# Scan and gated MLP on one core: two pairs turned by DMA instead of TensorE, and loads and stores moved to GpSimd's queue

## The chip, the cores and the metric

One core of a Trainium2 chip. The metric is the device time of one execution in microseconds (us), as the median of several runs. The profile is one execution taken apart by the hardware profiler; its times are counted from the start of its span. Engines go by the profile's names: PE is TensorE's matmul, PEld its weight load, DVE is VectorE, ACT is ScalarE, POOL is GpSimd, SP is SyncE, which computes nothing here and issues DMAs.

## What is computed

A state-space scan over 4 batches, 8 heads and 768 positions (head width 32, state width 16), then a gated MLP over the 3072 tokens of 256 features:

```
for each chunk c of the positions:
    cum = cumsum(log a)                         # within the chunk
    M = (C B^T) * exp(cum_i - cum_j) * causal
    y = M x + (C state) * exp(cum_i)
    state = exp(sum log a) * state + sum_j B_j x_j exp(cum_last - cum_j)
tokens = y, heads side by side                  # 3072 x 256
out = (relu(tokens w_gate) * (tokens w_val)) w_out   # d_ff = 1536
```

Inputs and output are float32; the kernel multiplies in bf16.

## The kernel before, in words

The scan works in 12 pairs (p), each of two chunks of 128 positions (i = 0, 1) of one batch, all 8 heads at once; three pairs make a batch. The MLP works in 6 blocks (b) of 512 tokens, so block b needs pairs 2b and 2b + 1. In the loop over blocks (lines 968 to 1136), P = 2b + 2, Q = 2b + 3 and W = 2b + 1: while block b goes through the MLP, the pairs of the next block go through the scan. Each engine executes its instructions in the order of the program (`in_order`, line 15); that order is written out by hand, so whatever stands behind a waiting instruction waits too. DMAs issued by SP go through one queue and those issued by GpSimd through another.

A pair passes these steps:

- **Load** (`load`, line 102): C and B (two DMAs each of 64 KB in rows of 64 bytes, for pairs from 4 on) and x (two of 128 KB in rows of 128 bytes). The raw tiles have four buffers each.
- **Scaling**: B and C are multiplied by the decay factors `fac`. Pairs 0 to 5 use `scale_bc` or `scale_one` (lines 334 and 348) into a tile `bs`. Pairs 6 to 11 use `scale_padded` (line 292), which writes a zeroed tile `bz` (three of them, used in turn) with B in part 0, all of C in part 1 and C split by even and odd heads in parts 2 and 3.
- **Turning**, positions to heads x states. Pairs up to 5: `turn` (line 912), four TensorE transposes (line 389) into PSUM, then `tevac`: ScalarE copies B (`BT`, line 318), VectorE scales C twice with 0/1 masks (`CT`, line 415). Pairs from 6 on: one DMA transpose of the `bz` tile on SP's queue (`TT`, line 306).
- **x cast** to bf16 (`to_x`, line 358), on GpSimd or ScalarE.
- **G** = B C^T on TensorE (line 452, or 491 from pair 6 on) into four PSUM banks; **gevac** (line 458) moves it to the tile `gs` with the causal mask. ScalarE copies half q = 0 and part of q = 1, GpSimd masks these in place (`causal`, line 171, two instructions for a pair), VectorE does the rest.
- **inter** (lines 619, 670): C times the carried state; **Dm** (lines 630, 683): `gs` times x, into y. Dm waits for the masks of GpSimd. **states** (lines 569, 698) sums B^T x for the next pairs.
- **yevac** writes y to `yT`, the MLP's input.

Pairs from 6 on take G, inter and Dm two pairs at a time. In the MLP, `gv` and `gvh` compute gate and value products (lines 743, 758), ScalarE applies relu, VectorE multiplies, `fout` (line 788) makes the output product and `foevac` (line 806) copies it to an `ob` tile and stores it from SP.

What stands around the change on GpSimd, in order: in block 0, masks of pairs 2 and 3, scalings of pair 4 (`scale_one`, line 353); in block 1, C of pair 4, scaling of pair 5 (line 344) and its x cast, scaling of pair 6 (line 297, two copies of line 303) and its x cast, masks of pair 4, masks of pair 5, scaling and x cast of pair 7; in block 2, the small state products (`Sn`, line 722), scaling and x cast of pair 8, scaling of pair 9, masks of pair 6, masks of pair 7, state products. SP issues, from block 0's end: C of pair 4, a store, C, B and x of pair 5, a store, all of pair 6, all of pair 7, the transpose of pair 6, all of pair 8, two stores, the transpose of pair 7, all of pair 9, the transposes of pairs 8 and 9.

Of the kernel before, what the change touches and what calls it, by code (L numbers as in the profile page):

```python
# [11 lines left out]
ALU = mybir.AluOpType  # L12
# [17 lines left out]
def kernel(  # L30
# [13 lines left out]
    nc = tc.nc  # L44

    NB, NH, S, D = x.shape
    N = B.shape[-1]
# [26 lines left out]
    def place(p):  # L74
        b, c0 = p // PPB, 2 * (p % PPB)
        return b, c0, slice(c0 * 128, (c0 + 2) * 128)
# [215 lines left out]
    def scale_padded(p, eng):  # L292

        b, c0, _ = place(p)
        z = turned[p % 3]
        f = fac[:, b, c0:c0 + 2].rearrange("s i j h -> s i (j h)")
        eng.tensor_tensor(  # L297
            out=z.rearrange("s (i k) (h n) -> s i (k h) n", k=4, n=N)[:, :, 0:2 * NH],
            in0=st[p]["bcr"].rearrange("s i j h n -> s i (j h) n"),
            in1=f.to_broadcast([128, 2, 2 * NH, N]), op=ALU.mult)  # L300
        parts = z.rearrange("s (i k) (q t n) -> s i k t q n", k=4, q=4, t=2)
        for t in range(2):
            eng.tensor_copy(out=parts[:, :, 2 + t, t], in_=parts[:, :, 1, t])
        st[p]["B"] = [z[:, 4 * i] for i in range(2)]
        tt = st[p]["TT"] = att.tile([128, 8, 128], BF16, tag="TT", name="TT", bufs=4)
        nc.sync.dma_start_transpose(out=tt, in_=z.rearrange("s k n -> s (k n)"))

    def new_bs(p):
        st[p]["bs"] = att.tile([128, 4, 128], BF16, tag="bs", name="bs", bufs=6)
# [38 lines left out]
    def scale_one(p, eng, j):  # L348

        b, c0, _ = place(p)  # L350
        for i in range(2):
            f = fac[:, b, c0 + i, j].rearrange("s (t q) -> s t q", t=2)
            eng.tensor_tensor(
                out=st[p]["bs"][:, 2 * i + j].rearrange("s (q t n) -> s t q n", q=4, t=2),
                in0=st[p]["bcr"][:, i, j].rearrange("s (t q) n -> s t q n", t=2),
                in1=f.to_broadcast([128, 2, 4, N]), op=ALU.mult)
# [60 lines left out]
    def ct(p, i, rows=slice(0, 128), t=None):  # L417
        if p < NWIDE:
            c = st[p]["CT"][rows, :, :, 64 * i:64 * i + 64]
        else:  # L420
            c = st[p]["CT"][rows, :, i]
        return c if t is None else c[:, t]

    def split(p, ap):

        return ap.rearrange("s t (r m) -> s t r m", r=2) if p < NWIDE else ap
# [17 lines left out]
    def G(p):  # L444
        s = st[p]
        if "gp" not in s:
            G_banks(p)
        g = s["gp"]
        for i in range(2):
            for q in range(4):  # L450
                r = slice(32 * q, 32 * q + 32)
                nc.tensor.matmul(  # L452
                    out=split(p, g[q][:, i]), lhsT=s["BT"][r, i], rhs=ct(p, i, r),
                    start=(i == 0), stop=True, tile_position=(32 * q, 0),
                    skip_group_check=True)
        s["gs"] = att.tile([128, 4, 4, 128], BF16, tag="gs", name="gs", bufs=2)
# [336 lines left out]
    def fout_last(b):  # L793

        r0 = b * 512 + 384
        for m in range(2):
# [6 lines left out]
            (nc.vector.tensor_copy if m else nc.scalar.copy)(out=ob, in_=o)  # L803
            (nc.sync if m else nc.scalar).dma_start(out=out[r0:r0 + 128, ms], in_=ob)

    def foevac(b, ts, o=None):
        last = b == NBLK - 1 and ts == 2
        if ts % 2 == 0 and not last:
            return
        ob = ffn.tile([128, 2, DM], FP32, tag="ob", name="ob", bufs=3)  # L810
        r0 = b * 512 + ts * 128
        if last:
            nc.scalar.copy(out=ob[:, 0], in_=fst["o"][:, 0])
            nc.scalar.dma_start(out=out[r0:r0 + 128, :], in_=ob[:, 0])
            return
        nc.scalar.copy(out=ob, in_=o or fst["o"])  # L816
        rows = out[r0 - 128:r0 + 128, :].rearrange("(i p) m -> p i m", p=128)
        for part in ((slice(0, 1), slice(1, 2)) if b in (2, 3) and ts == 3 else (slice(0, 2),)):
            nc.sync.dma_start(out=rows[:, part], in_=ob[:, part])


    B_, C_ = slice(0, 1), slice(1, 2)
# [145 lines left out]
    for b in range(NBLK):  # L968
        P, Q, W = 2 * b + 2, 2 * b + 3, 2 * b + 1
        more = P < NPAIR  # L970
        if b == 1:
            load(P + 2, nc.sync)
            load(P + 3, nc.sync)
        if b == 2:
            scale(Q, nc.gpsimd)
            load(Q + 2, nc.sync)

        nh = (4, 6, 8, 0)[min(b, 3)]
        for f in range(nh):
            if b == 0:  # L980
                continue
            turning = f == (3 if b == 1 else nh - 3)
            gvh_mm(b, f, 0)
            gvh_relu(b, f, 0)
            gvh_mul(b, f, 0)
            if b == 1 and f == 1:
                to_x(P, nc.scalar)
            if turning:
                inter(W, 0)
                inter(W, 1)  # L990
                Dm(W)
                if b == 1:
                    states(P)
                    scale_one(P, nc.gpsimd, 1)
                else:
                    states_two((P, Q))
                yevac(W, nc.scalar)
                if b == 1:
                    spread(P)
                else:  # L1000
                    sums_two((P, Q))
        for f in range(nh):
            gvh(b, f, 1)
        if b == 2:
            scale(P + 2, nc.gpsimd)
        for f in range(nh, NF):
            gv(b, f, b > 2 and f == 0)
            if b == 0:
                if f == 5:
                    over_sum(de_ps)  # L1010
                if f == 7:
                    sevac(1, 1)
                if f == 9:
                    turn(P)
                    tevac(P, nc.scalar, nc.vector)
                if f == 10:
                    held(Q, bc=False)
                if f == 11:
                    back(P)
                    backevac(P, nc.scalar)  # L1020
            elif b == 1:
                if f == nh:
                    turn(P)
                    tevac(P, nc.scalar, nc.vector)
                    scale(Q, nc.gpsimd)
                if f == 8:
                    turn(Q)
                    tevac(Q, nc.scalar, nc.vector)
                    scale(Q + 1, nc.gpsimd)
                    load(Q + 3, nc.sync)  # L1030
            elif b == 2:
                if f == 9:
                    scale_padded(Q + 2, nc.gpsimd)
                    load(Q + 3, nc.sync)
                    load(Q + 4, nc.sync)
            elif b == 3:
                if f in (2, 6):
                    scale(P + 2 + f // 4, nc.gpsimd)
# [3 lines left out]
        if b == 0:  # L1042

            for third in range(3):
# [16 lines left out]
                if third == 1:  # L1061
# [11 lines left out]
            A_ps[0] = rest  # L1073
            Dm(P)
            states(Q)
            held(Q + 2)
            fout(b, 3, range(4))
            inter(P, 0)
            inter(P, 1)
            gevac(Q, after={2: lambda: [yevac_half(P, t, nc.scalar) for t in range(2)],  # L1080
                            3: lambda: spread(Q)})
            new_bs(Q + 1)
            scale_one(Q + 1, nc.gpsimd, 0)
            fout(b, 3, range(4, NF))
            foevac(b, 3)
            continue
        elif b == 1:
            fout(b, 0)
            G(P)
            gevac(P)  # L1090
            over_sum2(de)
            fout(b, 1)
            foevac(b, 1)
            fout(b, 2)
        elif more:
            ahead = (P + 2, Q + 2) if Q + 2 < NPAIR else ()
            fout(b, 0, range(9), True)
            G_rows(P)
            opened = y_banks()
            inter_rows(P, opened)  # L1100
            inter_rows(Q, opened)
            gevac(P)
            fout(b, 0, range(9, NF))
            fout(b, 1)
            first_two = fst["o"]
            fout(b, 2, range(1))
            G_rows(Q)
            gevac(Q)
            if b == 2:
                to_x(Q + 2, nc.scalar)  # L1110
            foevac(b, 1, first_two)
            fout(b, 2, range(1, NF))
            fout(b, 3, range(8))
            Dm_two((P, Q))
            states_two(ahead)
            yevac_two((P, Q))
            sums_two(ahead)
            fout(b, 3, range(8, NF))
            foevac(b, 3)
            continue  # L1120
# [48 lines left out]
```

## Time and profile before

| | |
|---|---|
| median of 3 runs | 121.95 us (121.88 to 122.23) |
| the profiled execution | 121.95 us |
| its span, first to last instruction | 120.2 us |
| PE busy | 115.2 us, 96% of the span |
| DVE, ACT, POOL busy | 88.2, 76.7, 51.0 us |
| DMA traffic | 13.69 MB in 80591 packets, 73424 of them under 512 bytes |
| granted TensorE clock | 1.000 |

The page gives busy shares, the span in 40 slices of 3 us with the busy share in tenths, the chain of work that ended last followed back from the end, and the costliest groups of instructions. The timeline lists one engine's instructions in order of time, neighbours of a kind merged; in square brackets stands the idle time before them and what seems to have ended it. The table by stretches gives, for each stretch, the busy time of each engine, the granted clock, the DMA share (packet time over the time of 16 engines, which passes 1 where packets overlap) and GB/s. A wait for several semaphores is put down to one of them, which need not be the one that held it.

### The profile page before, as it was taken

What the parts mean: (1) busy time and instruction counts of PE and PEld (TensorE: products, weight loads), DVE (VectorE), ACT (ScalarE), POOL (GpSimd) and SP (SyncE); (2) the same over time, 40 slices, a digit from 0 to 9 for tenths busy, and PEclk for the clock granted to TensorE, in tenths of its full rate; (3) what the DMA queues carried; (4) which work ended last, traced back from release to release, by engine and by line L of the source; (5) the groups of instructions that cost most, each with busy time, mean ns of one, the idle gap of its engine ahead of it and who ended that gap; (6) DMA issues with size and microseconds to landing.
All of it is one profiled execution on the core that took longest, in us unless ns stands there. A gap on an engine that the chain in (4) does not pass through costs nothing.

```text
span 120.2 us, 3321 instructions
## 1 busy us (share of the span) xinstructions
PE 115.2 (96%) x1230; PEld 74.8 (62%) x1237; DVE 88.2 (73%) x208; ACT 76.7 (64%) x168; POOL 51.0 (42%) x103
## 2 busy tenths in 40 slices
PE   7988999999999999999999999999999999999990
PEld 2445854677885577887578544578444677444790
DVE  5898879976899866899775787856787775678400
ACT  4257887787998726888626776535767445767240
POOL 6879999744405181956055261633400033000000
PEclk9999999999999999999999999999999999999999
DMA  3999999989959897999995799942200002200022
GB/s 70 209 182 148 202 193 207 211 126 132 163 53 194 98 125 107 135 140 212 126 177 113 72 129 116 281 95 87 87 5 0 0 0 93 87 0 0 0 87 87
DMA packets 80591, 13.69 MB, mean 114 GB/s; under 512 B 73424, under 2 KB 80576, under 8 KB 80576
## 3 DMA queue, kind: packets, MB, share of 16 engines
q1 hardware_dynamic: 73088, 10.54, 54.6%
q0 software_dynamic: 4080, 2.36, 13.9%
q10 hardware_dynamic: 3408, 0.59, 2.6%
q8 instruction: 9, 0.15, 0.5%
q14 instruction: 6, 0.05, 0.1%
HBM read 11.12 MB, written 3.15 MB: 119 GB/s over the span
## 4 chain that ended last, share of the span: by engine, by line
PE 93%; DVE 3%; issue 1%; ACT 0%
PE o L788 26%; PE gate L743 19%; PE val L743 19%; PE gv L758 13%; PE w L200 3%; PE g L491 2%; PE g L452 2%; DVE bs L344 1%; PE y L683 1%; PE y L630 1%; PE o L800 1%; PE tp L389 1%; PE y L619 1%; PE bt L433 1%; PE dw L236 0%
## 5 line engine op out<-in xcount | busy, mean ns | idle before, releaser
L747 DVE TENSOR_TENSOR h<-r,val 128x512 bf16<-128x512 bf16 x54 | 36.9, 686 | 9.1 <-ACT r L746 6.6
L746 ACT ACTIVATE r<-gate 128x512 bf16<-128x512 f32 x54 | 32.2, 597 | 11.9 <-PE gate L743 11.2
L788 PE MATMUL o<-wo,h 128*128 128x256 bf16 x276 | 33.8, 273 | 0.0
L743 PE MATMUL gate<-yT,wg 128*128 128x512 bf16 x105 | 32.0, 379 | 0.2
L743 PE MATMUL val<-yT,wv 128*128 128x512 bf16 x105 | 31.5, 379 | 0.2
L788 PEld LDWEIGHTS <-h 128*128 128x128 bf16 x276 | 25.7, 98 | 5.4 <-issue 1.2
L171 POOL TENSOR_SCALAR_AFFINE_SELECT gs<-gs 128x512 bf16<-128x512 bf16 (+1 forms) x24 | 12.2, 531 | 20.7 <-ACT gs L464 20.7
L475 DVE TENSOR_TENSOR gs<-g,masks 128x512 bf16<-128x512 f32 x24 | 15.4, 685 | 6.0 <-PE g L491 2.8
L743 PEld LDWEIGHTS <-wv 128*128 128x128 bf16 x108 | 10.5, 98 | 12.6 <-DMA wv<-in_moe_w_val_dram 0.3
L743 PEld LDWEIGHTS <-wg 128*128 128x128 bf16 x108 | 10.4, 98 | 11.1
L768 DVE TENSOR_TENSOR h<-r,gv 128x256 bf16<-128x256 bf16 x36 | 14.2, 417 | 1.3 <-ACT r L765 1.1
L765 ACT ACTIVATE r<-gv 128x256 bf16<-128x256 f32 x36 | 13.6, 388 | 1.2
L464 ACT CAST gs<-g 128x512 bf16<-128x512 f32 x12 | 7.0, 586 | 11.4 <-PE g L491 5.8
L758 PE MATMUL gv<-yT,wg 128*128 128x256 bf16 x72 | 13.9, 273 | 0.0
L758 PE MATMUL gv<-yT,wv 128*128 128x256 bf16 x72 | 13.9, 273 | 0.0
L297 POOL TENSOR_TENSOR bz<-bcr,fac 128x512 bf16<-128x512 f32 x6 | 6.3, 1058 | 11.9 <-DMA bcr<-in_B_dram 6.8
L816 ACT COPY ob<-o 128x512 f32<-128x512 f32 x11 | 6.5, 590 | 4.2 <-PE o L788 4.1
L318 ACT CAST yT<-y 128x256 bf16<-128x256 f32 (+1 forms) x11 | 5.4, 515 | 4.9 <-PE y L683 2.8
L758 PEld LDWEIGHTS <-wv 128*128 128x128 bf16 x72 | 7.0, 98 | 0.9
L758 PEld LDWEIGHTS <-wg 128*128 128x128 bf16 x72 | 6.7, 98 | 1.0 <-issue 0.2
L318 POOL CAST xb<-xr 128x512 bf16<-128x512 f32 (+1 forms) x8 | 4.7, 592 | 3.9 <-DMA xr<-in_x_dram 3.9
L200 PE MATMUL w<-const-bfloat16-1.0 128*128 128x512 bf16 (+3 forms) x14 | 5.0, 482 | 0.8 <-PEq L1153 0.8
(120 smaller groups left out, 110.4 us busy)
## 6 DMA issues: line engine op xcount, KB each, us to landing
xr<-in_x_dram SPq DMA_DIRECT2D x24, 128.0 KB, 3.3
out_dram<-ob SPq DMA_DIRECT2D x9, 256.0 KB, 2.5
bcr<-in_B_dram SPq DMA_DIRECT2D x16, 64.0 KB, 3.0
bcr<-in_C_dram SPq DMA_DIRECT2D x16, 64.0 KB, 3.0
wg<-in_moe_w_gate_dram POOLq DMA_DIRECT2D x6, 128.0 KB, 4.8
wv<-in_moe_w_val_dram POOLq DMA_DIRECT2D x6, 128.0 KB, 5.1
wo<-in_moe_w_out_dram POOLq DMA_DIRECT2D x3, 256.0 KB, 6.8
out_dram<-ob SPq DMA_DIRECT2D x4, 128.0 KB, 2.2
```

Of the source, the lines that this page charges most:

```text
L171: nc.gpsimd.affine_select(out=dst, in_=dst, pattern=pattern, compare_op=ALU.is_ge, fill=0.0, base=0, channel_multiplier=-1)
L200: nc.tensor.matmul(out=w[:, 0:cols], lhsT=nc.const_aps.tensor(1.0, [128, 128], BF16), rhs=nc.const_aps.tensor(1.0, [128, cols], BF16), sta ...
L318: (eng.copy if eng is nc.scalar else eng.tensor_copy)(out=out, in_=in_)
L464: nc.scalar.copy(out=d[:, 0], in_=g[0])
L475: nc.vector.tensor_tensor(out=d[:, q], in0=g[q], in1=m, op=ALU.mult)
L743: nc.tensor.matmul(out=o, lhsT=w_tile(ws, f, k), rhs=yT[:, k, tk], start=(k == 0), stop=(k == 1), skip_group_check=True)
L746: nc.scalar.activation(r, g, AF.Relu)
L747: nc.vector.tensor_tensor(out=fst[b][:, f], in0=r, in1=v, op=ALU.mult)
L758: nc.tensor.matmul(out=gv_[:, j], lhsT=w_tile((wgs, wvs)[j], f, k), rhs=yT[:, k, tk], start=(k == 0 and not (early and j)), stop=(k == 1), ...
L765: nc.scalar.activation(r[:, 0:256], fst[b, f, u][:, 0], AF.Relu)
L768: nc.vector.tensor_tensor(out=fst[b][:, f, u * 256:(u + 1) * 256], in0=fst.pop((b, f, u, "r"))[:, 0:256], in1=fst.pop((b, f, u))[:, 1], op ...
L788: nc.tensor.matmul(out=o[:, ts % 2], lhsT=fst[b][:, f, ts * 128:(ts + 1) * 128], rhs=wo[:, f], start=(f == 0 and new), stop=(f == NF - 1), ...
```

## The change

- Pairs 4 and 5 are scaled by a new `scale_turned` into the padded `bz` tiles (four GpSimd instructions for a pair: B by even and odd heads, then C by even and odd heads) and turned by a DMA transpose on SP's queue. Their `turn` and `tevac` go; G, inter and states read `TT` and `bz`.
- GpSimd issues three stores (both of block 0 and the last of block 1, that one held back to block 2) and x of pairs 6 and 8.
- On GpSimd, the x cast of pair 6 moves from ahead of the masks of pair 4 to behind them, and the x cast of pair 8 from ahead of pair 9's scaling to between the masks of pairs 6 and 7.
- SP issues the transpose of pair 4 between B and x of pair 5, and that of pair 5 behind B of pair 6. Stores of blocks 2 to 5 go out in halves.

The core of the diff:

```
+    def scale_turned(p, eng):
+        b, c0, _ = place(p)
+        z = turned[p % 3]
+        dst = z.rearrange("s (i k) (q t n) -> s i k t q n", k=4, q=4, t=2)
+        src = st[p]["bcr"].rearrange("s i j (t q) n -> s i j t q n", t=2)
+        f = fac[:, b, c0:c0 + 2]
+        for j in range(2):
+            for t in range(2):
+                eng.tensor_tensor(
+                    out=dst[:, :, j * (2 + t), t], in0=src[:, :, j, t],
+                    in1=f[:, :, j, 4 * t:4 * t + 4].to_broadcast([128, 2, 4, N]), op=ALU.mult)
+        st[p]["B"] = [z[:, 4 * i] for i in range(2)]
+    def turn_padded(p):
         tt = st[p]["TT"] = att.tile([128, 8, 128], BF16, tag="TT", name="TT", bufs=4)
-        nc.sync.dma_start_transpose(out=tt, in_=z.rearrange("s k n -> s (k n)"))
+        nc.sync.dma_start_transpose(out=tt, in_=turned[p % 3].rearrange("s k n -> s (k n)"))
...
-        for part in ((slice(0, 1), slice(1, 2)) if b in (2, 3) and ts == 3 else (slice(0, 2),)):
-            nc.sync.dma_start(out=rows[:, part], in_=ob[:, part])
+        if b == 1 and ts == 3:
+            late_store.append(lambda: nc.gpsimd.dma_start(out=rows, in_=ob))
+            return
+        for part in ((slice(0, 1), slice(1, 2)) if b > 1 else (slice(0, 2),)):
+            (nc.sync if b else nc.gpsimd).dma_start(out=rows[:, part], in_=ob[:, part])
...
         if b == 1:
-            load(P + 2, nc.sync)
+            new_bc(P + 2)
+            load_bc(P + 2, 1, nc.sync)
+            load_bc(P + 2, 0, nc.sync)
+            scale_turned(Q, nc.gpsimd)
+            turn_padded(Q)
+            new_x(P + 2)
+            for i in range(2):
+                load_x(P + 2, i, nc.gpsimd)
             load(P + 3, nc.sync)
+            to_x(Q, nc.gpsimd)
         if b == 2:
             scale(Q, nc.gpsimd)
+            late_store.pop()()
+            new_x(P + 2)
+            for i in range(2):
+                load_x(P + 2, i, nc.gpsimd)
             load(Q + 2, nc.sync)
...
         if b == 2:
-            scale(P + 2, nc.gpsimd)
+            scale_padded(P + 2, nc.gpsimd)
...
-                if f == nh:
-                    turn(P)
-                    tevac(P, nc.scalar, nc.vector)
-                    scale(Q, nc.gpsimd)
                 if f == 8:
-                    turn(Q)
-                    tevac(Q, nc.scalar, nc.vector)
-                    scale(Q + 1, nc.gpsimd)
-                    load(Q + 3, nc.sync)
+                    scale_padded(Q + 1, nc.gpsimd)
+                    new_bc(Q + 3)
+                    load_bc(Q + 3, 1, nc.sync)
+                    load_bc(Q + 3, 0, nc.sync)
...
-            held(Q + 2)
+            held(Q + 2, with_x=False)
...
-            new_bs(Q + 1)
-            scale_one(Q + 1, nc.gpsimd, 0)
+            scale_turned(Q + 1, nc.gpsimd)
+            turn_padded(Q + 1)
+            new_x(Q + 2)
+            for i in range(2):
+                load_x(Q + 2, i, nc.sync)
...
             G(P)
             gevac(P)
+            to_x(P + 2, nc.gpsimd)
...
             first_two = fst["o"]
+            if b == 2:
+                to_x(P + 2, nc.gpsimd)
             fout(b, 2, range(1))
             G_rows(Q)
             gevac(Q)
```

More of the change, by code (lines that the diff above doesn't have):

```diff
@@ L304, in scale_padded @@
         st[p]["B"] = [z[:, 4 * i] for i in range(2)]
+        turn_padded(p)
+    def scale_turned(p, eng):
[11 more added lines that the diff above has]
+    def turn_padded(p):
         tt = st[p]["TT"] = att.tile([128, 8, 128], BF16, tag="TT", name="TT", bufs=4)
-        nc.sync.dma_start_transpose(out=tt, in_=z.rearrange("s k n -> s (k n)"))
+        nc.sync.dma_start_transpose(out=tt, in_=turned[p % 3].rearrange("s k n -> s (k n)"))
     def new_bs(p):
@@ L420, in ct @@
         else:
-            c = st[p]["CT"][rows, :, i]
+            c = st[p]["TT"][rows, 4 * i + 2:4 * i + 4]
         return c if t is None else c[:, t]
@@ L452, in G @@
                 nc.tensor.matmul(
-                    out=split(p, g[q][:, i]), lhsT=s["BT"][r, i], rhs=ct(p, i, r),
+                    out=split(p, g[q][:, i]), rhs=ct(p, i, r),
+                    lhsT=s["BT"][r, i] if p < NWIDE else s["TT"][r, 4 * i],
                     start=(i == 0), stop=True, tile_position=(32 * q, 0),
@@ L804, in fout_last @@
             (nc.sync if m else nc.scalar).dma_start(out=out[r0:r0 + 128, ms], in_=ob)
+    late_store = []
     def foevac(b, ts, o=None):
@@ L993 @@
                     states(P)
-                    scale_one(P, nc.gpsimd, 1)
                 else:
```

## The prediction

> **What bounds the kernel now.** I read the page first: the busy shares and the chain of work that ended last.
>
> ```profile
> PE 115.2 (96%) x1230; PEld 74.8 (62%) x1237; DVE 88.2 (73%) x208; ACT 76.7 (64%) x168; POOL 51.0 (42%) x103
> ...
> DMA  3999999989959897999995799942200002200022
> ...
> PE 93%; DVE 3%; issue 1%; ACT 0%
> ```
>
> TensorE carries 93% of the chain, so time taken from its stream counts in full, and time taken from VectorE or ScalarE counts only where TensorE waits for them. The waits of TensorE and its weight loads from 16 us on hold nothing over 0.3 us in one place. The DMA row is the second thing to see: it stands mostly at 8 or 9 from 3 us to 63 us. The transfers have little room in the blocks that the change touches.
>
> Next, the timeline of TensorE around the two turns that go (columns: start, duration, engine, line, operation; durations overlap, so a step is the distance from one start to the next).
>
> ```profile
> 36.49 0.59 PE L743 MATMUL val<-yT,wv 128*128 128x512 bf16 x2
> 36.92 0.39 PE L389 MATMUL tp<-ident,bs 128*128 128x128 bf16 x4
> 37.15 0.59 PE L743 MATMUL gate<-yT,wg 128*128 128x512 bf16 x2
> ...
> 38.87 0.39 PE L389 MATMUL tp<-ident,bs 128*128 128x128 bf16 x4
> 39.09 0.59 PE L743 MATMUL gate<-yT,wg 128*128 128x512 bf16 x2
> ```
>
> The turns take 37.15 - 36.92 = 0.23 us and 39.09 - 38.87 = 0.22 us, with no idle time around them.
>
> **The change, part by part.**
>
> Removed from TensorE: eight transposes of pairs 4 and 5 (the built order of instructions has 16 rows fewer on PE, eight weight loads and eight matmuls): 0.23 + 0.22 = **0.45 us** of the chain. G, inter and states of the two pairs read other tiles with the same counts and columns: nothing.
>
> Removed beside it: two BT copies on ScalarE (0.37 us each) and four CT scalings on VectorE (0.34 us each). TensorE runs at its full pace of 0.43 us for two 512-column matmuls behind both turns, so this is worth nothing now.
>
> GpSimd's arithmetic: four L353 scalings (0.40 us) and two L344 scalings (0.62 us), 2.8 us, become eight of L353's size, 3.2 us. The B half of pair 4 is still written first, before the states of block 1 at 32.36 us (0.76 us from 29.94 us on): nothing.
>
> GpSimd's DMA issues: three stores and four x loads, seven in all. Its weight loads (L153) held the engine for 0.776 and 0.739 us each. The store rows, 256 of 1 KB, are like those; the first fits into the idle 1.55 us ahead of the masks at 28.93 us, the second into the wait of 4.51 us for B of pair 5. An x load has 1024 rows of 128 bytes, which no GpSimd row shows: from 0.78 us (the issue alone counts) to 3.1 us (four times the rows). I take 1 us, since the three L161 loads with twice the bytes cost the same 0.770 us, and SP's own issue of x, with a median of 0.62 us, is short too. The Trainium skill ("DMA: Bandwidth & Descriptors", Anatomy of one DMA — SWDGE (gpsimd) path) holds that many descriptors can be issued before their cost shows; by it the term would stay near the lower end, and no run here shows it yet.
>
> The two new DMA transposes: two undisturbed ones of before, issued at 75.77 and 77.18 us and landing 3.2 and 2.9 us later, are 1.1 us apart at landing. So each takes some **1.1 us of the stream of transfers**, 2.2 us together. Their own deadlines hold: that of pair 4 stands behind the B loads of pair 5 in SP's queue, is issued near 34 us and lands within 5.1 us (the longest of before), by 39 us; inter needs it at 41.24 us. That of pair 5 is issued near 40.7 us, lands by 45.8 us at the latest, and G needs it at 46.74 - 0.45 = 46.29 us.
>
> What the 2.2 us push back matters at two places, both on GpSimd, where a scaling that waits for a load stands ahead of the masks that TensorE needs. Block 1:
>
> ```profile
> 41.76 1.06 POOL L297 TENSOR_TENSOR bz<-bcr,fac 128x512 bf16<-128x512 f32 x1 [2.41 <-DMA bcr<-in_B_dram]
> 42.88 0.52 POOL L303 COPY bz<-bz 128x128 bf16<-128x128 bf16 x2
> 43.56 0.61 POOL L318 CAST xb<-xr 128x512 bf16<-128x512 f32 x1 [0.16 <-DMA xr<-in_x_dram]
> 44.45 1.00 POOL L171 TENSOR_SCALAR_AFFINE_SELECT gs<-gs 128x512 bf16<-128x512 bf16 x2 [0.28 <-ACT gs L464]
> ```
>
> B of pair 6 lands at 41.6 us (38.83 + 2.8). Scaling to masks done takes 0.16 + 1.64 + 1.00 = 2.8 us behind it, since the cast moves behind the masks. Dm of pair 4 starts at 46.37, with the gain at 45.92 us. So it is hidden while B lands by **43.1 us**. Ends: 41.6 + 1.1 (one transpose) - 1.4 (two stores out of SP's queue, 0.64 and 0.86 us of issue with what lies between) = 41.3; with everything in one stream, x of pair 6 (1.9 us from B's landing to x's) ahead of it too, 44.6 us. Block 2:
>
> ```profile
> 61.27 1.06 POOL L297 TENSOR_TENSOR bz<-bcr,fac 128x512 bf16<-128x512 f32 x1 [5.13 <-PE y L670]
> 62.39 0.52 POOL L303 COPY bz<-bz 128x128 bf16<-128x128 bf16 x2
> 62.87 1.01 POOL L171 TENSOR_SCALAR_AFFINE_SELECT gs<-gs 128x512 bf16<-128x512 bf16 x2
> 64.24 1.00 POOL L171 TENSOR_SCALAR_AFFINE_SELECT gs<-gs 128x512 bf16<-128x512 bf16 x2 [0.36 <-ACT gs L464]
> ```
>
> The view names PE, but the scaling of pair 9 starts 0.2 us after its B load lands (58.19 + 2.9 = 61.1 us), and no late PE instruction touches its tiles, so I read it as that load. The new cast of x of pair 8 stands between the two pairs of masks: load to last mask is 0.2 + 1.60 + 0.97 + 0.57 + 1.00 = 4.35 us. The last mask is needed by the fourteenth of the 32 matmuls at 65.59 us, near 65.84, or 65.39 us with the gain. So here B must land by **61.05 us**: there is no slack if the load stays where it was. Ends: 61.1 + 2.2 = 63.3 us, if all transfers share one stream; with x of pairs 6 and 8 and the stores gone from SP's queue and costing it nothing, some 57 us.
>
> Which end? This table shows stretches with and without GpSimd's own queue in use (its weight loads run in the first); the last two numbers are the DMA share and GB/s.
>
> ```profile
> 11.50:16.00 4.50, 4.50 (x72) 3.73 (x72) 3.77 (x10) 4.09 (x17) 4.50 (x8) 1.00 1.48 198
> ...
> 36.00:45.00 9.00, 8.95 (x71) 5.48 (x70) 7.17 (x15) 5.77 (x12) 4.55 (x8) 1.00 1.00 139
> ```
>
> With two queues the engines carried 1.48, with SP's alone 1.00. So SP's queue does not fill them, and work moved to the second queue costs the first less than its full time: at 1.4 shared equally, some 0.43 of it (half of 1.4 is 0.7 of SP's pace for W/0.7, so SP loses 0.3/0.7 of W). Then B of pair 6 lands at 41.6 + 1.1 + 0.43 x 1.9 - 0.57 x 1.4 = 42.7 us, hidden by 0.4; and B of pair 9, with 5.9 us moved (x 2 x 1.9, stores 3 x 0.7), at 61.1 + 2.2 - 0.57 x 5.9 = 59.9 us, hidden by 1.1.
>
> Other edits: stores of later blocks in halves add an SP issue of 0.37 us; the last stands at 115.42 us and the queue is idle until 117.78 us. x of pair 8 keeps GpSimd some 3 us from 51 us on; its Sn results are wanted only near 60.9 us. Nothing for either.
>
> Sum: -0.45 us. The profiled execution took 121.95 us with a span of 120.2 us, 1.75 us lying around it, and equals the median of the runs. 121.95 - 0.45 = **121.50 us**.
>
> **The rivals.**
>
> *Slower: the load of B of pair 9 comes late in block 2.* Each us past 61.05 us costs TensorE one. At 61.5 us the gain is just spent; past 61.9 us the kernel is slower by over 0.3%. For it: SP's x loads issued at 14.39 and 16.22 us landed 10.1 us later (median) beside GpSimd's weights, against 3.3 us otherwise, and the slack is nothing. Against it: the 1.48. Two thirds of the way from 59.9 to 63.3, I take 62.2 us: masks at 66.55, +0.7 us, **122.65 us**; at the bound 63.3 us, 123.75 us. The Trainium skill ("DMA: Bandwidth & Descriptors", Issuing engines are not separate DMA queues) says that all issuers end on the same 16 engines and that a second one saves issue time alone: by that rule the answer is near the bound; the share of 1.48 disagrees in part, the 10.1 us agrees.
>
> *About the same: one of the two waits appears, but smaller than the gain.* B of pair 6 at 43.5 us (0.4 late), or of pair 9 at 61.4: **121.9 us**.
>
> *GpSimd itself is late: x loads at 3.1 us each.* The scaling of pair 5 ends near 38.1 us; 38.1 + 6.2 + 0.61 + 1.64 + 1.00 = 47.55 against 45.92 us: +1.6 - 0.45, **123.1 us**. It decides from about 2.5 us an issue on.
>
> That the transposes stay is excluded by the built order.
>
> **How the numbers follow.** Forecast 0.48, about the same 0.22, late load 0.22, long issue 0.08. A measurement of this kernel tells some 0.3% (0.37 us) from no change. The forecast's gain is only just over that: I give 0.06 of its 0.48 to within. Faster 0.42, same 0.28, slower 0.30. The range runs from 121.3 us (runs of before spread 0.35 us) to 122.7 us, which takes in the late load at its middle; the upper half of that and the long issue stay out.
>
> **What would show it.** Right: no L389 matmuls after 30 us; the scaling of pair 6 starts before 43.3 us, that of pair 9 before 61.2 us; TensorE shows no wait for GpSimd's masks at the first Dm of block 1 or the Dm of block 2; DMA share over 1.1 where GpSimd's x loads run. Wrong: a gap ahead of those Dm matmuls ended by POOL gs, x issues on GpSimd of over 2.5 us, or TensorE waiting for TT.

## The result, and the profile after

The changed kernel took 123.02 us (median of 22 runs, 122.13 to 124.05) beside 122.14 us for the kernel before on the same chip (22 runs, 121.83 to 122.88): a ratio of 1.006 with a 95% interval of 1.0044 to 1.0077. It is **slower by 0.6%**, some 0.7 us; the ratio is one of means, and leaves out the one run of after (124.05 us) that fell into a slower state. The forecast was 121.5 us. The profiled execution of after took 122.8 us with a span of 121.1 us, against 120.2 us before.

The page of after, the lines that answer to those of before:

```profile
PE 115.6 (95%) x1222; PEld 74.6 (62%) x1229; DVE 87.6 (72%) x204; ACT 76.0 (63%) x166; POOL 57.0 (47%) x112
...
DMA  3999999989979999999696679993300002200022
...
PE 72%; DMA 10%; POOL 9%; SPq 3%; DVE 2%; issue 2%; ACT 1%; POOLq 0%
PE o L806 21%; PE gate L761 15%; PE val L761 14%; PE gv L776 10%; DMA wo<-in_moe_w_out_dram 7%; DMA bcr<-in_B_dram 3%; PE w L200 3%; POOL wg L153 2%; POOL wv L153 2%; SPq L92 2%; PE g L509 2%; POOL gs L171 2%; PE y L701 1%; PE o L818 1%; PE y L648 1%
```

TensorE has its eight matmuls fewer, and it is still busy for 95% of the span. In the chain, DMA, GpSimd and SP's queue now make up 22%, but that is the path behind a wait and not time lost: the largest piece (7%) is the load of `wo`, which landed at 25.82 us, ahead of anything the change does to TensorE; only the load of B, SP's queue and GpSimd's masks (3, 2 and 2%) lead to the change. The loss is read from TensorE's timeline. The timeline of TensorE at the first turn shows the gain (columns as in the prediction):

```profile
36.57 0.38 PE L761 MATMUL gate<-yT,wg 128*128 128x512 bf16 x1
37.00 0.59 PE L761 MATMUL val<-yT,wv 128*128 128x512 bf16 x2
37.43 0.59 PE L761 MATMUL gate<-yT,wg 128*128 128x512 bf16 x2
```

Val to gate is 37.43 - 37.00 = 0.43 us; before, 0.66 us with the turn between them. The time comes back in block 1, as the timelines of GpSimd (three lines) and of TensorE show there:

```profile
44.57 1.05 POOL L297 TENSOR_TENSOR bz<-bcr,fac 128x512 bf16<-128x512 f32 x1 [3.08 <-DMA bcr<-in_B_dram]
45.68 0.52 POOL L303 COPY bz<-bz 128x128 bf16<-128x128 bf16 x2
46.16 1.00 POOL L171 TENSOR_SCALAR_AFFINE_SELECT gs<-gs 128x512 bf16<-128x512 bf16 x2
```

```profile
46.85 0.27 PE L648 MATMUL y<-gs,xb 128*32 128x128 bf16 x5 [0.35 <-POOL gs L171]
```

B of pair 6 landed at 44.34 us. Its scaling starts at 44.57 (41.76 before), the masks end at 47.16, and TensorE, which could have begun Dm of pair 4 at 46.43 us, stands for 0.35 us ahead of it and again inside it. In block 2 there is little more (GpSimd's timeline; the copies are left out):

```profile
62.46 1.06 POOL L297 TENSOR_TENSOR bz<-bcr,fac 128x512 bf16<-128x512 f32 x1 [4.85 <-DMA bcr<-in_B_dram]
...
64.06 1.01 POOL L171 TENSOR_SCALAR_AFFINE_SELECT gs<-gs 128x512 bf16<-128x512 bf16 x2
65.02 0.62 POOL L335 CAST xb<-xr 128x512 bf16<-128x512 f32 x1
65.58 1.02 POOL L171 TENSOR_SCALAR_AFFINE_SELECT gs<-gs 128x512 bf16<-128x512 bf16 x2
```

B of pair 9 landed at 62.30 us, against 61.06 before; the last mask ends at 66.60 us, and Dm loses 0.09 us.

The whole difference of these two executions can be added up by laying the two traces side by side: the start of the same TensorE instruction in both, after minus before. That **offset** is +0.51 us at 34 us, in front of anything the change does to TensorE; +0.06 behind the two turns (-0.45); +0.79 behind Dm of pair 4 (+0.73); +0.88 behind Dm of block 2 (+0.09) and until the end. The first 0.51 us is not the change's: e3 below is the same program as after until 39 us, and stands at -0.08 us at 34 us; e10 is the same as before until block 2, and stands at +0.65.

### The profile page after: what moved, and what is told of

Read it like the earlier page. It is cut to its first block, busy times and chain, and to the rows that moved or that the text cites. A ratio compares the mean times of both kernels' runs of the same rounds, so it can differ in the third digit from the quotient of the medians.

```text
span 121.1 us, 3310 instructions
## 1 busy us (share of the span) xinstructions
PE 115.6 (95%) x1222; PEld 74.6 (62%) x1229; DVE 87.6 (72%) x204; ACT 76.0 (63%) x166; POOL 57.0 (47%) x112
## 4 chain that ended last, share of the span: by engine, by line
PE 72%; DMA 10%; POOL 9%; SPq 3%; DVE 2%; issue 2%; ACT 1%; POOLq 0%
PE o L806 21%; PE gate L761 15%; PE val L761 14%; PE gv L776 10%; DMA wo<-in_moe_w_out_dram 7%; DMA bcr<-in_B_dram 3%; PE w L200 3%; POOL wg L153 2%; POOL wv L153 2%; SPq L92 2%; PE g L509 2%; POOL gs L171 2%; PE y L701 1%; PE o L818 1%; PE y L648 1%
```

## The experiments

**Theory.** The loads of SP's queue set the time. The transfers were full before, and the change puts two transposes into them and does not get from the second queue what the prediction booked. Late loads cost time only at *gates*, as this text calls places where GpSimd stands waiting for a load with work behind it that TensorE needs next. There are two in series, block 1 (B of pair 6) and block 2 (B of pair 9). **Rivals:** the wait in block 1 is the whole loss; or the load on SP's queue comes from the transposes alone, or from GpSimd's x loads alone.

In the cuts of the edits, `...` stands for lines left out, and the comments at line ends are added here. Every experiment in one table. Offsets against the first profile of before: at 9 us, behind the turns (40 us), behind Dm of pair 4 (48), behind the sums of pairs 6 and 7 (60), behind Dm of block 2 (67). "Landed" is the second half of each load. All in us.

| kernel | ratio (95%) | 9 | 40 | 48 | 60 | 67 | B 6 landed | x 7 | B 9 |
|---|---|---|---|---|---|---|---|---|---|
| before | 1 | 0 | 0 | 0 | 0 | 0 | 41.60 | 48.95 | 61.06 |
| e0, before again | (one run, 121.87 us) | -0.08 | -0.08 | -0.08 | -0.08 | -0.08 | 41.84 | 48.75 | 61.67 |
| after | 1.006 (1.0044 to 1.0077) | 0.13 | 0.06 | 0.79 | 0.79 | 0.88 | 44.34 | 50.91 | 62.30 |
| e1 | 1.0113 (1.0068 to 1.0158) | 0.46 | 0.06 | 0.06 | 0.06 | 4.16 | 43.78 | 50.59 | 64.08 |
| e2 | 0.9988 (0.996 to 1.0017) | 0.01 | 0.03 | 0.03 | 0.59 | 0.59 | 44.76 | 51.40 | 63.24 |
| e3 | 1.0172 (1.0116 to 1.0227) | -0.10 | -0.53 | -0.32 | 0.50 | 1.89 | 43.21 | 50.93 | 63.30 |
| e4 | 1.0284 (1.0239 to 1.033) | 0.29 | -0.16 | 0.12 | 1.50 | 3.70 | 43.71 | 52.31 | 65.02 |
| e5 | 1.0095 (1.0056 to 1.0134) | 0.46 | 0.46 | 0.46 | 0.46 | 2.34 | 43.71 | 49.19 | 63.67 |
| e6 | 1.0061 (1.0025 to 1.0096) | 0.46 | 0.01 | 1.65 | 1.65 | 1.65 | 44.57 | 47.76 | 64.06 |
| e7 | 1.0137 (1.0082 to 1.0192) | 0.45 | 0.05 | 0.27 | 0.83 | 2.34 | 43.80 | 51.56 | 63.75 |
| e8 | 0.9956 (0.9925 to 0.9987) | 0.45 | 0.02 | 0.02 | 0.24 | 0.24 | 44.17 | 49.98 | 62.26 |
| e9 | 1.0011 (0.9981 to 1.0042) | 0.00 | 0.50 | 0.50 | 0.73 | 1.52 | 44.95 | 51.99 | 62.86 |
| e10 | 1.0031 (1.0002 to 1.0061) | 0.49 | 0.65 | 0.65 | 0.87 | 0.87 | 42.37 | 49.40 | 62.43 |
| e11, e8 again | 1.0001 (0.9981 to 1.0021) | -0.18 | 0.22 | 0.22 | 0.44 | 0.44 | 44.32 | 50.58 | 62.77 |

In the profile of e1 the granted clock was 0.53 from 68 to 70 us and 0.84 from 70 to 75 us, where the other profiles have 0.995 to 1.0 on the mean, so its 4.16 us holds more than the wait. The expectation of e0 failed: it stands at -0.08 us and not at 0.2 to 0.6; e3 and e10 show that the beginnings differ all the same.

The rows add up as far as one profile can: the gain of 0.45 us and the losses at the gates add up to +2.0, +3.4 and +1.8 us for e3, e4 and e7, where the ratios say +2.1, +3.5 and +1.7. For after, e2, e5, e6 and e9 the one profile and the ratio differ by 0.3 to 0.7 us, so a single profile's sum is no better than that.

**e1, the first gate alone.** In after's block 1, the scaling of pair 6 moves behind GpSimd's masks of pair 4.

```diff
-                    scale_padded(Q + 1, nc.gpsimd)      # at f == 8
...
             gevac(P)
+            scale_padded(Q + 1, nc.gpsimd)
```

> One edit of the changed kernel: on GpSimd the scaling of pair 6 (and with it its transpose on SP's queue) stands behind the masks of pair 4 instead of ahead of them. Theory of two gates in series: the wait of TensorE at the Dm of pair 4 (0.7 us in the changed kernel's trace) goes, but the load of B of pair 9 still lands at 62 us or later, and with the cast of x of pair 8 between the masks those of pair 7 still end near 66.5 us, so that the Dm of block 2 now waits 0.7 to 1.2 us: time 0.0 to 0.6 us over the kernel before. Rival, one gate: only the Dm of pair 4 counts, and the kernel is 0.4 us faster than before. Rival, the cost lies elsewhere (start, longer issues): 0.6 us or more over before, as the changed kernel.

The wait in block 1 is gone (48 us: 0.06), and the kernel is no faster: the time is lost in block 2, where B of pair 9 landed at 64.08 us. The time itself, 1.4 us over before, is beyond the theory's 0.0 to 0.6 us and in the range of "the cost lies elsewhere"; it is the place of the loss that speaks for the theory. The load also came 1.8 us later than in after: the edit moves the transpose of pair 6 on SP's queue from 47.53 to 51.33 us, so that two transposes stand shortly ahead of pair 9's loads (51.33 and 53.80 us); that this is the reason was not tried. The waits of TensorE:

```profile
PE y L701 <- POOL gs L171: 1.8, 2, 0.9
```

The first rival (block 1 is the whole loss) falls. In after, the wait in block 1 had hidden the second gate: TensorE was late already when it got there.

**e2, both gates.** e1, with the cast of x of pair 8 moved up, and the scaling of pair 9 placed between the masks of pairs 6 and 7.

```diff
-                    scale_padded(Q + 2, nc.gpsimd)      # at f == 9
+                    to_x(P + 2, nc.gpsimd)
...
             if b == 2:
-                to_x(P + 2, nc.gpsimd)
+                scale_padded(Q + 2, nc.gpsimd)
```

> The edit of the run above, and in block 2 the cast of x of pair 8 stands ahead of pair 6's masks and the scaling of pair 9 between the masks of pairs 6 and 7. Two gates: no wait of TensorE for GpSimd over 0.1 us at either Dm, and the eight transposes' 0.45 us come out: 0.3 to 0.45 us faster than before. One gate: the same time as the run above. Cost elsewhere: no better than 0.2 us over before.

Neither Dm waits any more, though B of pair 9 landed at 63.24 us, 2.2 us later than in before. What is left is a third gate that the theory had not named: x of pair 7 landed at 51.40 us, and its cast is needed for the sums of pairs 6 and 7. It costs 0.56 us, so the gain of 0.3 to 0.45 us that was expected did not come out; the ratio says 0.15 us, within the noise of before. GpSimd and TensorE in the timeline:

```profile
51.52 0.62 POOL L335 CAST xb<-xr 128x512 bf16<-128x512 f32 x1 [0.39 <-DMA xr<-in_x_dram]
...
52.19 0.24 PE L716 MATMUL A_ps<-xb,bz 128*32 128x64 bf16 x8 [0.38 <-POOL xb L335]
```

**e4 and e5, the halves of the change.** e4 has the transposes, with x of pairs 6 and 8 and the stores back on SP; e5 has GpSimd's issues in the kernel before, with the turns still on TensorE.

```diff
-            (nc.sync if b else nc.gpsimd).dma_start(out=rows[:, part], in_=ob[:, part])
+            nc.sync.dma_start(out=rows[:, part], in_=ob[:, part])
...
-                load_x(P + 2, i, nc.gpsimd)     # twice: block 1 and block 2
+                load_x(P + 2, i, nc.sync)
```

> The changed kernel with x of pairs 6 and 8 and the three stores issued by SP again, x of pair 6 behind the transpose of pair 5; the transposes and the order of scalings, casts and masks stay. If the two transposes push the loads back by their own time: B of pair 6 lands at 42.7 us or later (41.6 in the trace of before plus 1.1), B of pair 9 at 62.5 to 63.5 us, and the time is 0.3 to 1.5 us over before, most of it waited for at the Dm of block 2. If GpSimd's x loads, sharing the engines with SP's loads, are what made B of pair 6 late: B of pair 6 lands by 43.0 us, no wait at the Dm of pair 4, and what is left comes from block 2 alone.

> The kernel before with the GpSimd issues alone (x of pairs 6 and 8, three stores, the halved stores, the casts where the change puts them), pairs 4 and 5 still turned by TensorE. If GpSimd's x loads delay SP's: B of pair 6 lands past 43.0 us without any new transpose, and the time is 0.2 to 0.9 us over before. If the transposes alone did it: B of pair 6 lands by 42 us, no wait at either Dm, and the time is that of before within 0.2 us.

Both are slower than before, by 3.5 and 1.2 us, and both beyond the ranges expected of them (1.5 and 0.9 us at most). The transposes alone are slower than both halves together; the moves alone (1.0056 to 1.0134) are not told apart from after (1.0044 to 1.0077). The waits of TensorE in e4 (first fence) and in e5:

```profile
PE y L701 <- POOL gs L171: 1.3, 2, 0.9
PE A_ps L716 <- POOL xb L335: 1.2, 1, 1.2
```

```profile
PE y L683 <- POOL gs L171: 0.9, 1, 0.9
```

With the transposes alone, x of pair 7 and B of pair 9 come 3.4 and 4.0 us later than in before, so the transposes load the stream. But e5, without one new transpose, has B of pair 9 at 63.67 us too: x of pair 8, which SP had issued at 50.94 us in before, goes out on GpSimd at 52.30 us, then runs beside the transpose of pair 7, which takes 9.0 us to land (5.1 us in before), and C and B of pair 9 stand behind that one. So neither rival about one half holds: both halves push B of pair 9 past the gate, and with the transposes there the second queue earns part of their cost back (1.028 to 1.006).

This holds beyond the two. In the nine profiles with x of pair 8 on GpSimd, the transpose of pair 7 landed 5.9 to 9.0 us after its issue, and the four loads of C and B of pair 9 took 4.0 to 7.2 us to issue; in the five without (before, e0, e4, e9, e10) it is 4.7 to 5.3 and 2.9 to 4.1 us.

**e3, x of pair 6 back on SP,** behind the transpose of pair 5, all else as in after.

```diff
-                load_x(P + 2, i, nc.gpsimd)     # block 1
+                load_x(P + 2, i, nc.sync)
```

> After, with x of pair 6 alone back on SP's queue, behind the transpose of pair 5; x of pair 8 and the three stores stay on GpSimd. Theory (two gates on one full stream): B of pair 6 no longer shares the engines with x's 256 KB, which at the 180 GB/s of that stretch are 1.45 us, and lands at about 42.9 us where it landed at 44.34; no wait before Dm of pair 4 (0.0 to 0.2 us where it was 0.7). But nothing is taken from the stream ahead of B of pair 9, which still lands at 62.0 to 62.8 us, and the masks of pair 7 then wait 0.6 to 0.9 us more than they did: 122.6 to 123.2 us, ratio 1.004 to 1.008. First rival (the first wait is the whole loss, block 2 has room): 122.3 us, ratio 0.999 to 1.002. Second rival (it is the DMA transposes and the store ahead of it that make B of pair 6 late, not the sharing): B of pair 6 stays at 44 us and the time at 123.0 us or more.

B of pair 6 landed at 43.21 us, 3.58 us behind its issue (4.17 in after), and the wait in block 1 fell to 0.2 us. Half of the 1.13 us by which B came sooner is the beginning (0.59 us), the other half fits a sharing of the engines with x. Over all profiles the sharing is plainer: B took 3.5 to 4.2 us to land in the nine with x of pair 6 on GpSimd, and 2.8 to 3.0 in the other four than e3. But the time rose to 1.0172, more than the theory gave, since against TensorE's own pace the loads are now later at both later gates (0.8 us lost at the sums, 1.4 us in block 2; the expectation had left the sums out). So the second queue is no cure, but x of pair 6 on it is worth some 1.1% of the time (1.4 us, 0.7 to 2.0 by e3's interval), which the theory in its pure form (only the sum of transfers counts) does not give. Its two issues held SP's queue in e3 for 43.40 - 42.15 = 1.25 us, which is about as much.

**e7, one transpose more.** Pair 5's is done twice, into a spare tile.

```diff
             turn_padded(Q)
+            spare = att.tile([128, 8, 128], BF16, tag="TTd", name="TTd", bufs=1)
+            nc.sync.dma_start_transpose(out=spare, in_=turned[Q % 3].rearrange("s k n -> s (k n)"))
```

> After, with one DMA transpose more: pair 5's, done a second time into a spare tile that nothing reads, right behind the first. It adds no arithmetic and no wait, only 1.1 us of transfers (the estimate on record for one transpose). Theory (the stream is full from 36 to 61 us): C and B of pair 7, x of pair 7 and B of pair 9 all land about 1.1 us later (B of pair 9 at 63.4 rather than 62.3) and the time grows by 0.9 to 1.2 us: 123.9 to 124.2 us, ratio 1.013 to 1.017. Rival (what cost is GpSimd's queue, the transposes are light, for the stream has room): B of pair 9 lands 0.0 to 0.4 us later and the time grows by 0.3 us at most, ratio 1.005 to 1.009.

The second landed at 45.83 us, 1.04 us behind the first, and held SP's queue for 44.32 - 42.97 = 1.35 us:

```profile
40.74 2.18 SPq L323 DMA_TRANSPOSE TT<-bz  x1
42.97 1.31 SPq L1001 DMA_TRANSPOSE TTd<-bz  x1
44.32 1.20 SPq L92 DMA_DIRECT2D bcr<-in_C_dram  x2
```

B of pair 9 landed 1.45 us later than in after; the ratio went from 1.006 to 1.0137, some 0.9 us (0.3 to 1.6 by e7's interval). A transfer with no arithmetic and no reader costs about its whole time (0.9 to 1.2 us was expected). The rival's 0.3 us lies at the edge of that interval; its landing, 0.4 us later at most, is out.

**e6, x of pair 7 on GpSimd as well,** on top of e2, to open the third gate.

```diff
-            load(P + 3, nc.sync)
+            new_bc(P + 3)
+            load_bc(P + 3, 1, nc.sync)
+            load_bc(P + 3, 0, nc.sync)
+            new_x(P + 3)
+            for i in range(2):
+                load_x(P + 3, i, nc.gpsimd)
```

> The kernel with both gates opened (scaling of pair 6 behind the masks of pair 4, scaling of pair 9 between the masks of pairs 6 and 7, which took 122.36 us, 0.999) with x of pair 7 also issued by GpSimd, right behind x of pair 6. Theory: what was left there was the cast of x of pair 7 behind its load, 0.4 to 0.5 us at 51.6 us; on the second queue the load goes out at 41 us rather than 46.7 and lands by 49; the wait goes and the 0.45 us of the eight transposes stand: 121.7 to 122.0 us, ratio 0.994 to 0.998. Rival: the 1 KB rows of this x starve SP's loads of B and C of pair 7 (128-byte rows), whose scaling stands ahead of the same cast; the wait at 51.6 us stays or grows to 1 us: 122.4 to 123.0 us, ratio 1.000 to 1.006.

(Rows of x have 128 bytes and those of C and B 64; the expectation has them longer.) The third gate opened (x landed at 47.76 us), and a fourth shut that neither side had named; the time, 1.0061, is the upper end of the rival's range, and at another place than it said: the transpose of pair 5, beside four x loads of GpSimd, landed at 48.34 us, 6.6 us behind its issue (4.1 us in after). TensorE:

```profile
48.38 0.40 PE L469 MATMUL g<-TT 32*128 32x256 bf16 x8 [1.57 <-DMA TT<-bz]
```

**e8 and e11, three gates.** e2, with the sums of pairs 6 and 7 one unit of products later on TensorE; **e10** is the control, that last edit alone in the kernel before.

```diff
-                else:
-                    states_two((P, Q))
...
-                else:
-                    sums_two((P, Q))
+            if b > 1 and f == nh - 2:
+                states_two((P, Q))
+                sums_two((P, Q))
```

> The kernel with both gates opened (122.36 us, ratio 0.999), and with the sums of pairs 6 and 7 one unit of the first half's products later in block 2, that is 0.9 us later on TensorE, so that the cast of x of pair 7, done at 52.14 us, is no longer waited for. Theory (the transposes save 0.45 us, and each microsecond lost stands at a gate on a late load): no wait left between 36 and 70 us, offset 0.45 us lower than with that wait, 121.8 to 122.1 us, ratio 0.994 to 0.998. Rival (the loads slip by as much as TensorE gains, so that the next gate, the scaling of pair 9 or of pair 11, takes what this one gives): 122.2 to 122.6 us, ratio 0.998 to 1.002, with a wait of 0.3 us or more behind 60 us.

> The kernel before, with only the sums of pairs 6 and 7 one unit later in block 2. In before, x of pair 7 lands at 48.9 us, 2.7 us ahead of them, so there is no wait to take away. Theory: no change, ratio 0.998 to 1.002, 122.2 to 122.6 us. Rival (the place of the sums matters by itself, for ScalarE or VectorE): a change of over 0.3% one way or the other; then what the three gates give can't be put down to the cast of x.

> The kernel with three gates opened, a second time, on whichever chip comes: it took 0.9956 of before with an interval of 0.9925 to 0.9987. If the 0.45 us of the eight transposes stand whenever no load is waited for, the ratio is 0.994 to 0.998 again and there is no wait over 0.2 us on TensorE between 36 and 70 us. Rival (the loads land near enough to the gates that an execution now and then waits): ratio 0.998 to 1.003, and a wait of 0.3 us or more in the profile.

Nothing on TensorE waits between 36 and 70 us in e8 and e11, though B of pair 9 lands as late as in after (62.26 us in e8). The chain of e8, and GpSimd in block 2:

```profile
PE 95%; DVE 2%; ACT 0%; issue 0%
```

```profile
62.11 1.01 POOL L171 TENSOR_SCALAR_AFFINE_SELECT gs<-gs 128x512 bf16<-128x512 bf16 x2 [2.82 <-ACT gs L482]
63.08 1.07 POOL L297 TENSOR_TENSOR bz<-bcr,fac 128x512 bf16<-128x512 f32 x1
...
64.69 1.00 POOL L171 TENSOR_SCALAR_AFFINE_SELECT gs<-gs 128x512 bf16<-128x512 bf16 x2
```

The masks are first, so the load is hidden. The same loads cost 0.82 us in after and 0 here; what differs is the order on GpSimd, and the later sums. The control missed its expectation of no change: 1.0031, just in its rival's range, and its profile shows that the later sums cost 0.22 us by themselves (0.65 to 0.87). So e8 and e11 pay that too: -0.45 + 0.22 = -0.23 us, or 0.998. The two measurements, 0.9956 and 1.0001, lie on both sides of it; the second is in the range of e11's rival, without the wait that this rival asked for. So this version is not shown to be slower than before, nor faster.

**e9, x of pair 8 behind B of pair 9 on SP,** on top of e1 with the later sums.

```diff
-                load_x(P + 2, i, nc.gpsimd)
-            load(Q + 2, nc.sync)
+            new_bc(Q + 2)
+            load_bc(Q + 2, 1, nc.sync)
+            load_bc(Q + 2, 0, nc.sync)
+            for p in (P + 2, Q + 2):
+                new_x(p)
+                for i in range(2):
+                    load_x(p, i, nc.sync)
```

> After, with the scaling of pair 6 behind the masks of pair 4, the sums of pairs 6 and 7 one unit later, and x of pair 8 back on SP, behind B of pair 9 (the scaling of pair 9 still ahead of both masks). Theory (what makes B of pair 9 late is x of pair 8, whose 1 KB rows GpSimd sends beside it): B of pair 9, at 64.1 us with x of pair 8 on GpSimd, lands at 61.5 to 62.5; the masks of pair 7 end by 67 us, the wait before Dm of block 2 falls from 2.7 us to 0.5 at most: 122.0 to 122.7 us, ratio 0.997 to 1.004. Rival (the lateness was piled up before 52 us, by the transposes of pairs 4 and 5 and x of pair 6): B of pair 9 still lands at 63.5 us or later and the wait stays over 1.5 us: 123.6 to 124.4 us, ratio 1.009 to 1.016.

(Here too the expectation says 1 KB rows; x has 128 bytes a row.) The time fell from e1's 1.0113 to 1.0011, inside the theory's range. Its profiled execution was one of its slowest (123.85 us, the median being 122.41) and still has 0.8 us of wait in block 2, with B of pair 9 1.2 us earlier than e1's, but at 62.86 us, not by 62.5. So x of pair 8 beside it is a part of that load's lateness; the rest comes from elsewhere, and no run here takes it apart.

## Why the prediction was wrong, point by point

- **The eight transposes, -0.45 us: right.** The offset falls by 0.44 to 0.46 us between 34 and 40 us in every kernel without them (0.51 to 0.06 in after; e5 and e10, which keep them, do not fall). The copies off ScalarE and VectorE gave nothing, as booked.
- **GpSimd's x issues, 1 us: right.** The group of the four in after (busy us, mean ns):

```profile
L100 POOL DMA_DIRECT2D xr<-in_x_dram x4 | 3.6, 899 | 0.0
```

  They took 0.88 to 0.93 us each, beside 0.74 to 0.78 for rows of 1 KB. The long-issue rival is out. The Trainium skill's sentence on many descriptors before their cost shows ("DMA: Bandwidth & Descriptors", Anatomy of one DMA — SWDGE (gpsimd) path) agrees with these durations.
- **1.1 us of stream a transpose: right** for the engines (1.04 us in e7), **but too little on SP's queue**: there pair 4's held 1.5 us in after (36.61 - 35.11) and pair 5's 2.35 (43.25 - 40.90). The deadlines of the two held in after (landed at 38.35 and 45.04 us), the second with 1.8 us to spare; e6 used that up.
- **The two places and their thresholds: right, within 0.2 us.** With the 0.51 us by which this execution began late, B of pair 6 had to land by 43.1 + 0.51 = 43.61 us; it came at 44.34, and 0.73 us were lost. B of pair 9 had to land by 61.05 + 0.51 + 0.73 = 62.29 us; it came at 62.30, and 0.09 us were lost. By the same sums B of pair 6 is 0.19, 0.32 and 0.20 us late in e3, e4 and e7, which lost 0.21, 0.28 and 0.22 us there; B of pair 9 is 1.30, 2.02 and 1.42 us late, and 1.39, 2.20 and 1.51 us were lost.
- **"Which end?": wrong, and this is the step that failed.** It read the DMA share of 1.48 beside GpSimd's weight loads as room that SP's queue leaves idle, booked moved work at 0.43 of its time, and so had B of pair 6 at 42.7 and B of pair 9 at 59.9 us. The trace of before already spoke against the reading. Its last GpSimd load lands at 25.00 us, and later SP's queue alone reaches as much (the last two columns are DMA share and GB/s):

```profile
55.00:56.00 1.00, 1.00 (x12) 0.90 (x10) 0.95 (x4) 0.85 (x3) 0.94 (x3) 1.00 1.45 237
```

  So 1.00 was no ceiling of one queue, and 1.48 no mark of a second. SP's queue in block 1 of after:

```profile
35.11 1.39 SPq L323 DMA_TRANSPOSE TT<-bz  x1
36.61 1.15 SPq L100 DMA_DIRECT2D xr<-in_x_dram  x2
37.80 1.66 SPq L92 DMA_DIRECT2D bcr<-in_C_dram  x2
39.51 1.29 SPq L92 DMA_DIRECT2D bcr<-in_B_dram  x2
```

  From 41.6 us in before: +0.5 for the late beginning; +1.5 for the transpose (36.61 - 35.11; booked 1.1); -0.86 for the second store, while the first saved nothing, since the issue of B of pair 5 starts no sooner for it (33.10 us, 32.68 in before; the two were booked together at -0.8, and the prediction's 0.64 and 0.86 add up to 1.5, not its 1.4); and **+1.4 for x of pair 6**, for B landed 4.17 us behind its issue beside GpSimd's x, and 2.76 us in before (booked 0.8). That is 44.1 of the 44.34 us. Of the 1.1 us by which B missed its booked time, the late beginning aside, 0.6 is x and 0.4 the transpose; by these sums x alone would have cost 0.2 us at the gate, and the transpose alone nothing. Of the 1.9 us booked for x on SP's queue, moving it saved 0.5 and not 1.1: in this execution it cost **0.74 of its time, not 0.43**. That size is not a constant: e7 is the same program up to there, and has 3.73 us, which is 0.51 of the time. In block 2, SP's queue before (first fence) and after:

```profile
55.88 1.46 SPq L92 DMA_DIRECT2D bcr<-in_C_dram  x2
57.38 1.39 SPq L92 DMA_DIRECT2D bcr<-in_B_dram  x2
58.82 1.33 SPq L100 DMA_DIRECT2D xr<-in_x_dram  x2
```

```profile
55.05 1.88 SPq L92 DMA_DIRECT2D bcr<-in_C_dram  x2
56.97 3.14 SPq L92 DMA_DIRECT2D bcr<-in_B_dram  x2
60.15 1.21 SPq L100 DMA_DIRECT2D xr<-in_x_dram  x2
```

  Here the queue did gain: with less to issue, it came to C of pair 9 at 55.05 us, 0.83 us sooner. Then it stood: C and B took 60.15 - 55.05 = 5.1 us to issue beside x of pair 8, and 2.9 us in before. The transposes and the moves together were booked at 2.2 - 3.4 = -1.2 us for B of pair 9; the late beginning aside, they came to +0.7. The runs do not split these 1.9 us between transposes that hold the queue longer and moves that relieve it less. The table by stretch for 36 to 45 us shows in after:

```profile
36.00:45.00 9.00, 8.95 (x66) 5.44 (x66) 6.76 (x13) 5.49 (x11) 4.29 (x8) 1.00 1.08 167
```

  The share is 1.08, not 1.48; while x of pair 6 is under way (39.1 to 44.1 us) it is 1.14, and 1.05 for x of pair 8 (52.6 to 59.4 us). The weights of the 1.48 came in packets of 512 bytes; GpSimd's x comes in packets of 4,096 bytes, beside SP's of 64 to 256, and the row did not carry over. That the packets are the reason is not shown. The rule that the prediction cited and gave the lesser chance (the Trainium skill, "DMA: Bandwidth & Descriptors", Issuing engines are not separate DMA queues: all issuers end on the same 16 engines) was the nearer one. By it a second queue saves the issue time alone; e3 agrees, with 1.25 us of issue and a gain of some 1.4 us. By the Trainium skill's same page (Queues, rings and completion order) each engine goes round the queues a packet at a time; no run here shows the turns.
- **The rivals.** "Slower" came true, and by a late load, but the profiled wait stood mostly at the first place, 0.73 us against a gain of 0.45. The prediction had both places as alternatives; in fact the first covers the second, and the third gate (x of pair 7 before the sums, 0.56 us in e2) was missed.
- **What one profile does not settle.** -0.45 + 0.73 + 0.09 = +0.37 us, and the runs say +0.7 (0.6%). A likely rest is block 2, where B of pair 9 differs by 0.6 us between two executions of before itself (61.06 and 61.67), and where after's profile has the second earliest B of all with x of pair 8 on GpSimd; that is argued from the table, and no run took it apart.

## What to carry to other kernels

A full row of DMA shares means that a new transfer has a price, and a second queue only a discount: measure the discount with transfers of the same kind, not with the weights of another stage. Then look for each engine that waits in order for a load with something urgent queued behind it, and move the urgent work in front; in e2 and e8 that took back the loss without a change of queue. List all such gates before costing one, since a wait at the first hides the next.

## What the runs showed of the hardware

- **An uneven beginning.** Programs that are alike so far reach 9 us at offsets from -0.18 to +0.49 us: e0 and e10 have -0.08 and +0.49, e8 and e11, one kernel, 0.45 and -0.18. At 34 us it is -0.08 (e0, e3) to +0.95 us (e9), and after's +0.51 grew mostly in between. A difference of 0.5 us between two profiles says nothing until this is taken off.
- **Holes in the transfers.** A 16 KB packet of the instruction queue, nine of them in a span, is often followed by a stretch with hardly a transfer. One came at 57.7 us in after, between the issues of the two loads of B of pair 9 (56.97 and 59.52 us); by stretch:

```profile
57.20:58.70 1.50, 1.45 (x8) 0.67 (x8) 1.26 (x3) 1.19 (x3) 0.41 (x2) 1.00 1.30 193
58.70:60.20 1.50, 1.50 (x9) 0.68 (x8) 1.15 (x3) 0.97 (x3) 0.00 (x0) 1.00 0.11 9
```

  The share falls from 1.30 to 0.11 for 1.5 us. In before, that stretch shows 1.01, and a like hole lies at 34.1 us. The hole is not what makes B of pair 9 late: e2, e3, e5 and e6 have shares of 0.86 to 1.36 in the same stretch, and B lands at 63.2 to 64.1 us there, later than in after. The Trainium skill ("Runtime: NRT & Kernel Launch", Instruction fetch mechanics) says that instructions are refilled in blocks of 16 KiB, which agrees with the packet; of a hole it says nothing, and that the packet makes it was not tried.
- **Transposes beside x loads.** DMA transposes landed 2.7 to 4.7 us after issue in e4, with all loads on SP's queue, and up to 5.1 us in before; beside GpSimd's x of pair 8 the transpose of pair 7 took from 5.9 (after) to 9.0 us (e5). Not every x load does this: beside x of pair 6 the transpose of pair 5 took 3.0 (e1) to 4.5 us (e11), and only beside four x loads 6.6 us (e6).
